# Finishing the last 256 tokens of the last projection as two groups of 128, in another order of products and with stores of 128 KB

## Chip, cores and metric

One core of one Trainium2 chip. The metric is device time in microseconds (us); of several executions the median is given. Each run is compared with the kernel before on its own chip.

## The reference

The computation normalises 2048 tokens of width 1024, runs a dilated local attention (32 heads, window 8) and a SwiGLU block of hidden width 3584 on them, and returns `x + s * g`:

```python
x = A_x
xn = _layernorm(x, axis=-1)
s = _A_ref(xn, A_wqkv, A_wo)          # ... attention, then "@ wo"
g = _silu(_B_ref(xn, B_w1, B_w3, B_w2))
return x + s * g
```

The change touches only the end of this: the projection `@ wo`, the product with the gate `g`, the addition of `x` and the store of the result.

## The kernel before

All large products use seven half-size products in place of eight (Strassen's scheme in Winograd's form): sums of blocks of both operands are made beforehand, seven products run on TensorE into PSUM, and partial results are copied from one PSUM accumulator to another (by ScalarE) or added (by VectorE). Tokens are handled in two batches of 1024 (`b`). Inside `wo`, a batch has two groups of 256 rows in each row half (`gp`), and a group gives four quadrants (`u` for the row half, `dh` for the column half): e11 is (0, 0), e12 is (0, 1), e21 is (1, 0) and e22 is (1, 1). "The last 256 tokens" are the group `b == 1, gp == 1`; strictly it covers 256 rows in each of the two row halves.

For the second batch's last group, VectorE adds `x` and SyncE issues a plain store. The other groups add onto an output that already holds `x`, by an accumulating store from GpSimd.

```python
def wo(b):
    # ... operands; for b == 1 the needed part of x is loaded into xw
        def product(ps, gp, lhs, rhs, first):
            for i in I:
                g = gp * 2 + i
                mm(ps[i], [lhs[:, j, g * P:(g + 1) * P] for j in range(4)], [rhs[:, j, :] for j in range(4)], first)

        both = lambda t: [t[:, i] for i in I]
        for gp in G2:
            run_hooks()
            last = b == 1 and gp == 1
            pa = bank2(f"wa{b}_{gp}")
            product(both(pa), gp, a11, b11, True)
            pe = bank2(f"we{b}_{gp}")
            product(both(pe), gp, s1, t1, True)
            flush()
            pb = [bank2(f"wb{b}_{gp}{i}")[:, i] for i in I] if last else bank2(f"wb{b}_{gp}")
            for i in I:
                if last:
                    act_copy(pb[i], pa[:, i])
            if not last:
                act_copy(pb[:], pa[:])
            pbs = pb if last else both(pb)
            sp5, su2 = k4(f"wsp{b}_{gp}"), k4(f"wsu{b}_{gp}")
            act_copy(sp5[:], pe[:])
            bg((7, 0)[gp] * (1 - b))
            product(pbs, gp, s2, t2, False)
            for i in I:
                if last:
                    act_copy(su2[:, i], pb[i])
            if not last:
                act_copy(su2[:], pb[:])
            product(both(pe), gp, s4, b22, False)
            finished(b, 0, 1, gp, pe, su2[:])
            product(pbs, gp, s3, t3, False)
            finished(b, 1, 1, gp, pb, sp5[:])
            product(both(pa), gp, a12, b21, False)
            finished(b, 0, 0, gp, pa)

            def tail(gp=gp, pb=pb, pbs=pbs):
                product(pbs, gp, a22, t4, False)
                finished(b, 1, 0, gp, pb)

            pend.append(tail)
```

```python
# ... out_rows (the rows of the output that a quadrant's group fills)
    def to_bf16(d, ps, add):
        if add is None:
            nc.scalar.copy(out=d, in_=ps[:])
        elif isinstance(ps, list):
            for i in I:
                nc.vector.tensor_add(d[:, i], ps[i], add[:, i])
        else:
            nc.vector.tensor_add(d, ps[:], add)

    # ...
    def finished(b, u, dh, gp, ps, add=None):
        g = g_tile(b, u, dh, gp)
        n = {(0, 0): 0, (1, 1): 2, (0, 1): 4, (1, 0): 0}[u, dh] + gp
        d = h_sb[:, 16 + 2 * n:18 + 2 * n, CH:]
        rows_ = out_rows(out_flat, b, u, dh, gp)
        with hp():
            if b == 0 or gp == 0:
                to_bf16(d, ps, add)
                anchor["v"] = nc.vector.tensor_mul(g, d, g)
                nc.gpsimd.dma_start(out=rows_, in_=g, accum_op=ALU.add)
            elif (u, dh) != (1, 0):
                to_bf16(d, ps, add)
                nc.vector.tensor_mul(g, d, g)
                nc.vector.tensor_add(g, g, xw[u, dh])
                nc.sync.dma_start(out=rows_, in_=g)
            else:
                for i in I:
                    if i == 0:
                        nc.scalar.copy(out=d[:, i], in_=ps[i])
                    nc.vector.tensor_mul(g[:, i], ps[i] if i else d[:, i], g[:, i])
                    nc.vector.tensor_add(g[:, i], g[:, i], xw[u, dh][:, i])
                    nc.sync.dma_start(out=rows_[:, i], in_=g[:, i])
```

Of the kernel before, what the change touches and what calls it, by code (L numbers as in the profile page):

```python
# [17 lines left out]
def kernel(  # L18
# [11 lines left out]
    nc = tc.nc  # L30
    P = 128
# [4 lines left out]
    CH = 512  # L36
# [9 lines left out]
    I = range(2)  # L46
# [4 lines left out]
    out_flat = out.rearrange("b s d -> (b s) d")  # L51
# [31 lines left out]
        out=ident[:], in_=ident[:], compare_op=ALU.not_equal, fill=1.0,  # L83
# [5 lines left out]
        out=ones4[:], in_=ones4[:], compare_op=ALU.is_ge, fill=0.0,  # L89
# [3 lines left out]
        out=ones4[:], in_=ones4[:], compare_op=ALU.is_ge, fill=0.0,  # L93
# [5 lines left out]
        out=maskb[0:32], in_=maskb[0:32], compare_op=ALU.is_ge, fill=-1.0e9,  # L99
# [7 lines left out]
    h_sb = keep.tile([P, FT, 2 * CH], BF16, name="h_sb")  # L107
# [3 lines left out]
    pb = keep.tile([P, W, P], BF16, name="pb")  # L111
# [20 lines left out]
    def bank2(name):  # L132
        return psum.tile([P, 2, CH], FP32, tag="mm", name=name)

    def k4(name, shape=(2, CH), dt=FP32):
        return kk.tile([P, *shape], dt, tag="k4", name=name)
# [10 lines left out]
    def mm(ps, lhs, rhs, first):  # L147
        n = len(lhs)
        for k in range(n):
            with behind("pe") if "open" in anchor else nullcontext():  # L150
                anchor["pe"] = nc.tensor.matmul(  # L151
                    ps, lhsT=lhs[k], rhs=rhs[k], start=(first and k == 0),
                    stop=(k == n - 1), skip_group_check=not first,
                )
# [4 lines left out]
    def act_copy(out_, in_):  # L159
        with hp():  # L160
            nc.scalar.copy(out=out_, in_=in_)  # L161
# [3 lines left out]
    def flush():  # L165
        while pend:
            pend.pop(0)()
# [51 lines left out]
    anchor = {}  # L219
# [7 lines left out]
    def behind(key):  # L227
        return tc.issue_after(anchor[key].ins) if key in anchor else nullcontext()
# [162 lines left out]
    def att_tile(shape, dt, name):  # L391
        return att.tile([P, *shape], dt, tag="a8", name=name)
# [109 lines left out]
    def run_hooks():  # L502
        while hooks:
            hooks.pop(0)()
# [43 lines left out]
    def bg(us):  # L548
        if us <= 0:
            return  # L550
        state_p[0] = tc.cur_priority
        pace["credit"] += us - pace["owed"]
        pace["owed"] = 0
        with priority(BG), behind("v"):
            while pace["credit"] > 0:
                t = next(att_it)
                if t is STOP:
                    pace["credit"] = min(pace["credit"], 6)
                    break
                else:  # L560
                    pace["credit"] -= t
# [15 lines left out]
    half = [0, 1]  # L577
# [7 lines left out]
    def release(key):  # L585
        free.extend(held.pop(key, []))
# [155 lines left out]
    G2 = range(2)  # L742
    gts = {}

    def g_tile(b, u, dh, gp):
        f0 = {(0, 0): 10, (1, 1): 10, (0, 1): 6, (1, 0): 6}[u, dh] + 2 * gp
        col = {(0, 0): 0, (1, 1): CH, (0, 1): 0, (1, 0): CH}[u, dh]
        return h_sb[:, f0:f0 + 2, col:col + CH]
# [133 lines left out]
    def wo(b):  # L882
        (a11, a12, a21, a22, s1, s2, s3, s4), (b11, b12, b21, b22, t1, t2, t3, t4) = wx[b]
        if b == 1:
            xt4 = att_tile((2, 2, 2, CH), BF16, "xw")
            for u in I:
                for dh in I:
                    xw[u, dh] = xt4[:, u, dh]
                    with behind("dl"):
                        nc.sync.dma_start(out=xw[u, dh], in_=out_rows(x_flat, 1, u, dh, 1))  # L890

        def product(ps, gp, lhs, rhs, first):
            for i in I:
                g = gp * 2 + i
                mm(ps[i], [lhs[:, j, g * P:(g + 1) * P] for j in range(4)], [rhs[:, j, :] for j in range(4)], first)

        both = lambda t: [t[:, i] for i in I]
        for gp in G2:
            run_hooks()
            last = b == 1 and gp == 1  # L900
            pa = bank2(f"wa{b}_{gp}")
            product(both(pa), gp, a11, b11, True)
            pe = bank2(f"we{b}_{gp}")
            product(both(pe), gp, s1, t1, True)
            flush()
            pb = [bank2(f"wb{b}_{gp}{i}")[:, i] for i in I] if last else bank2(f"wb{b}_{gp}")
            for i in I:
                if last:
                    act_copy(pb[i], pa[:, i])
            if not last:  # L910
                act_copy(pb[:], pa[:])
            pbs = pb if last else both(pb)
            sp5, su2 = k4(f"wsp{b}_{gp}"), k4(f"wsu{b}_{gp}")
            act_copy(sp5[:], pe[:])
            bg((7, 0)[gp] * (1 - b))
            product(pbs, gp, s2, t2, False)
            for i in I:
                if last:
                    act_copy(su2[:, i], pb[i])
            if not last:  # L920
                act_copy(su2[:], pb[:])
            product(both(pe), gp, s4, b22, False)
            finished(b, 0, 1, gp, pe, su2[:])
            product(pbs, gp, s3, t3, False)
            finished(b, 1, 1, gp, pb, sp5[:])
            product(both(pa), gp, a12, b21, False)
            finished(b, 0, 0, gp, pa)

            def tail(gp=gp, pb=pb, pbs=pbs):
                product(pbs, gp, a22, t4, False)  # L930
                finished(b, 1, 0, gp, pb)

            pend.append(tail)
        flush()
        release("wo")

    def out_rows(ap, b, u, dh, gp):
        g0 = ((2 * b + u) * NST + gp * 2) * P
        return ap[g0:g0 + 2 * P, dh * CH:(dh + 1) * CH].rearrange("(i p) n -> p i n", p=P)

    def to_bf16(d, ps, add):
        if add is None:
            nc.scalar.copy(out=d, in_=ps[:])
        elif isinstance(ps, list):
            for i in I:
                nc.vector.tensor_add(d[:, i], ps[i], add[:, i])
        else:
            nc.vector.tensor_add(d, ps[:], add)

    xw = {}  # L950

# [5 lines left out]
            with behind("sp"):  # L957
                nc.sync.dma_start(out=out_flat[r0:r0 + n, dh * CH:(dh + 1) * CH], in_=x_flat[r0:r0 + n, dh * CH:(dh + 1) * CH])

    def finished(b, u, dh, gp, ps, add=None):  # L960
        g = g_tile(b, u, dh, gp)
        n = {(0, 0): 0, (1, 1): 2, (0, 1): 4, (1, 0): 0}[u, dh] + gp
        d = h_sb[:, 16 + 2 * n:18 + 2 * n, CH:]
        rows_ = out_rows(out_flat, b, u, dh, gp)
        with hp():
            if b == 0 or gp == 0:
                to_bf16(d, ps, add)
                anchor["v"] = nc.vector.tensor_mul(g, d, g)
                nc.gpsimd.dma_start(out=rows_, in_=g, accum_op=ALU.add)
            elif (u, dh) != (1, 0):  # L970
                to_bf16(d, ps, add)
                nc.vector.tensor_mul(g, d, g)
                nc.vector.tensor_add(g, g, xw[u, dh])
                nc.sync.dma_start(out=rows_, in_=g)
            else:
                for i in I:
                    if i == 0:
                        nc.scalar.copy(out=d[:, i], in_=ps[i])
                    nc.vector.tensor_mul(g[:, i], ps[i] if i else d[:, i], g[:, i])
                    nc.vector.tensor_add(g[:, i], g[:, i], xw[u, dh][:, i])  # L980
                    nc.sync.dma_start(out=rows_[:, i], in_=g[:, i])



# [260 lines left out]
    with behind("dl"):  # L1245
        nc.sync.dma_start(out=xT[:], in_=x_dram[:])
        nc.sync.dma_start(out=xs[:], in_=xs_dram[:])
    wo(0)
    state.add("wo")
    mlp_up(1)  # L1250
    mlp_down(1, lambda: mid(1), (7, 10, 10, 9, 9, 3))
    wo(1)


# [28 lines left out]
```

## Time and profile before

| | kernel before |
|---|---|
| time, median of the first three executions | 723.84 us (723.78 to 724.5) |
| span in the profile | 721.8 us |
| TensorE busy | 710.0 us, 98% |
| first matmul of the last projection | 691.47 us |
| last matmul ends | 715.89 us |
| VectorE's last addition ends | 718.69 us |
| last store: issue begins | 718.85 us |
| end of the span | 721.8 us |

TensorE is busy for 98% of the span and its last matmul ends at 715.89, so what a change at this end can shorten without removing matmuls is the 5.9 us behind it. The prediction below shows the lines of that stretch. What the prediction does not show is how the kernel ends after the last store. The view of the waits on SyncE's queue, behind 717 us (who waited for whom: total in us, times, longest in us), has it:

```profile
SPq L1278 <- DMA out_dram<-h_sb: 1.1, 3, 0.5
SPq L981 <- DVE h_sb L980: 0.3, 1, 0.3
```

The second line is the last store waiting for VectorE's last addition. The first line is the closing of the program on SyncE: it waits until each store has landed, 1.1 us in all, 0.5 the longest. The landing of the last store is therefore part of the time, at full length.

### The profile page before, as it was taken

To read this page: it belongs to the slowest core of one execution; us is meant where nothing else is said; L and a number is where in the kernel's file an instruction comes from. 1 tells how busy PE (TensorE), PEld (TensorE's weight loads), DVE (VectorE), ACT (ScalarE), POOL (GpSimd) and SP (SyncE) were. 2 spreads that over 40 slices of the span, in tenths; PEclk is the share of its full clock that TensorE was granted. 3 is DMA by queue.
4 is the path that set the end of the run, shared out by engine and by line. 5 is a ranking of instruction groups with operands and counts; after the bars stand their busy time and mean duration, and the time that the engine had idled before them with its cause. 6 is when DMAs were issued, how large, how long until landed. Compare 5 with 4: busy or idle time off the path is not lost.

```text
span 721.8 us, 8746 instructions
## 1 busy us (share of the span) xinstructions
PE 710.0 (98%) x3313; PEld 346.2 (48%) x3367; DVE 624.9 (87%) x690; ACT 312.9 (43%) x326; POOL 95.7 (13%) x162
## 2 busy tenths in 40 slices
PE   8999999999999999999999999999999999999996
PEld 6655565654444444444444444444444444444442
DVE  7996879779879878978999999969859989999974
ACT  5745334356545456555555312034364573020233
POOL 0011100012300000233111000000435004000011
PEclk9999999999999999999999999999999999999999
DMA  9946257777754523558756547469799444563615
GB/s 337 275 125 182 82 185 228 258 249 238 246 172 153 191 71 117 173 191 268 246 174 216 190 132 250 144 205 385 168 276 336 139 138 150 168 202 129 199 36 108
DMA packets 119193, 139.51 MB, mean 193 GB/s; under 512 B 17648, under 2 KB 94448, under 8 KB 118512
## 3 DMA queue, kind: packets, MB, share of 16 engines
q1 hardware_dynamic: 104608, 97.01, 42.6%
q0 software_dynamic: 14544, 41.95, 18.0%
q8 instruction: 26, 0.43, 0.2%
q14 instruction: 15, 0.12, 0.1%
HBM read 96.21 MB, written 38.80 MB: 187 GB/s over the span
## 4 chain that ended last, share of the span: by engine, by line
PE 95%; ACT 2%; DVE 2%; issue 1%; DMA 0%; DVEq 0%; ACTq 0%
PE bm L151 20%; PE am L151 13%; PE em L151 13%; PE db L151 10%; PE bq L151 9%; PE de L151 7%; PE da L151 7%; PE eq L151 5%; PE aq L151 3%; PE wb L151 2%; PE af L151 2%; PE we L151 2%; PE wa L151 2%; DVE h_sb L236 1%; PE af L1049 1%
## 5 line engine op out<-in xcount | busy, mean ns | idle before, releaser
L151 PEld LDWEIGHTS <-wring 128*128 128x128 f16 (+1 forms) x1792 | 183.4, 102 | 204.3 <-issue 2.2
L151 PEld LDWEIGHTS <-h_sb 128*128 128x128 f16 (+1 forms) x1056 | 109.5, 104 | 118.4 <-issue 0.6
L151 PE MATMUL bm<-xs,wring 128*128 128x512 f16 x504 | 117.4, 379 | 0.2
L151 PE MATMUL am<-xT,wring 128*128 128x512 bf16 x322 | 79.0, 379 | 0.8
L151 PE MATMUL db<-wring,h_sb 128*128 128x512 f16 x336 | 73.2, 379 | 0.0
L481 DVE TENSOR_TENSOR BC<-Ep,vT 128x2048 bf16<-128x2048 bf16 x56 | 66.6, 1217 | 0.1
L426 DVE TENSOR_TENSOR pt<-qt,kT 128x4096 bf16<-128x4096 bf16 x24 | 54.9, 2290 | 0.6
L664 DVE TENSOR_TENSOR um<-em,um 128x1024 f32<-128x1024 f32 x28 | 34.2, 1222 | 21.0 <-PE em L151 13.3
L666 ACT ACTIVATE g<-um 128x1024 bf16<-128x1024 f32 x28 | 29.6, 1057 | 48.6 <-DVE um L664 48.6
L151 PE MATMUL da<-wring,h_sb 128*128 128x512 bf16 x219 | 48.7, 379 | 0.3
L467 POOL DMA_DIRECT2D Ep<-pb x64 | 38.0, 601 | 53.4 <-DVE pb L463 48.1
L151 PE MATMUL bm<-h_sb,wring 128*128 128x512 f16 x168 | 39.7, 379 | 0.0
L151 PE MATMUL em<-xs,wring 128*128 128x512 f16 x168 | 39.7, 379 | 0.0
L151 PE MATMUL em<-xT,wring 128*128 128x512 bf16 x161 | 39.2, 379 | 0.3
L491 DVE TENSOR_TENSOR oT<-oT,BC 128x2048 bf16<-128x2048 bf16 x32 | 39.0, 1219 | 0.3
L161 ACT COPY bm<-am 128x1024 f32<-128x1024 f32 x28 | 27.9, 998 | 25.9 <-PE am L151 25.9
L161 ACT COPY pm<-em 128x1024 f32<-128x1024 f32 x28 | 28.4, 1013 | 20.1 <-PE em L151 20.1
L161 ACT COPY um<-bm 128x1024 f32<-128x1024 f32 x28 | 28.4, 1014 | 18.9 <-PE bm L151 18.9
L685 ACT CAST g<-bm 128x1024 bf16<-128x1024 f32 x28 | 28.3, 1011 | 17.4 <-PE bm L151 17.4
L679 DVE TENSOR_TENSOR h_sb<-bm,pm 128x1024 bf16<-128x1024 f32 x21 | 25.6, 1218 | 5.1 <-PE bm L151 5.0
L489 DVE TENSOR_TENSOR BC<-BC 128x2048 bf16<-128x2048 bf16 x24 | 29.3, 1221 | 0.4
L428 DVE TENSOR_TENSOR pt<-pt 128x2048 bf16<-128x2048 bf16 x24 | 29.3, 1221 | 0.4
(197 smaller groups left out, 993.5 us busy)
## 6 DMA issues: line engine op xcount, KB each, us to landing
wring<-in_B_w_dram SPq DMA_DIRECT2D x61, 512.0 KB, 4.2
wring<-t_dram SPq DMA_DIRECT2D x16, 512.0 KB, 3.8
t_dram<-wring POOLq DMA_DIRECT2D x14, 512.0 KB, 3.8
wring<-t_dram SPq DMA_DIRECT2D x16, 384.0 KB, 4.9
wring<-in_B_w_dram SPq DMA_DIRECT2D x12, 384.0 KB, 4.5
wring<-in_A_x_dram SPq DMA_DIRECT2D x16, 256.0 KB, 4.2
Ep<-pb POOLq DMA_DIRECT2D x64, 64.0 KB, 4.9
wring<-in_A_wo_dram SPq DMA_DIRECT2D x8, 512.0 KB, 5.6
```

The lines of the kernel that those rows point to most:

```text
L151: anchor["pe"] = nc.tensor.matmul(ps, lhsT=lhs[k], rhs=rhs[k], start=(first and k == 0), stop=(k == n - 1), skip_group_check=not first,)
L161: nc.scalar.copy(out=out_, in_=in_)
L426: nc.vector.tensor_mul(p_t[:], q[:], kT[:, :, o:o + CH])
L428: nc.vector.tensor_add(p_t[:, 0:4, :], p_t[:, 0:4, :], p_t[:, 4:8, :])
L467: nc.gpsimd.dma_start(out=pr[c][r:P:NR, :, sq * P:(sq + 1) * P], in_=pb[sq * 32:(sq + 1) * 32, :, :])
L481: nc.vector.tensor_mul(dst, E[:, w, :].unsqueeze(1).to_broadcast([P, n, CH]), vT[:, js, o:o + CH])
L489: nc.vector.tensor_add(B, B, C)
L491: nc.vector.tensor_add(A, A, B if w0 else C)
L664: v = nc.vector.tensor_add(su2[:], pe[:], su2[:])
L666: nc.scalar.activation(out=hl["g"][:, :, CH:], in_=su2[:], func=ACTF.Silu)
L679: anchor["v"] = nc.vector.tensor_add(h[:, :, CH:], pb[:], sp5[:])
L685: nc.scalar.copy(out=hl["g"][:, :, 0:CH], in_=pb[:])
```

## The change

In the kernel before, the last group of 256 was split only in part: the accumulator `wb` had one PSUM tile for each 128 rows, and the copies around it and the last quadrant were done in halves. The change drops this and runs the last group as two complete groups of 128, so that the quadrants of the first half can be finished while TensorE works on the second. In these two groups e11 comes first, e22 second and e12 third (before: e12, e22, e11). All their stores are plain stores of 128 KB (before: three of 256 KB and two of 128 KB, plain too). The core of the diff (the lines that only pass `ii` on are cut):

```diff
-        def product(ps, gp, lhs, rhs, first):
-            for i in I:
+        def product(ps, gp, ii, lhs, rhs, first):
+            for n, i in enumerate(ii):
...
-        for gp in G2:
+        for gp, ii in ((0, I), (1, I)) if b == 0 else ((0, I), (1, (0,)), (1, (1,))):
...
-            product(both(pe), gp, s4, b22, False)
-            finished(b, 0, 1, gp, pe, su2[:])
-            product(pbs, gp, s3, t3, False)
-            finished(b, 1, 1, gp, pb, sp5[:])
-            product(both(pa), gp, a12, b21, False)
-            finished(b, 0, 0, gp, pa)
+            steps = {
+                "e12": lambda: (product(pe, gp, ii, s4, b22, False), finished(b, 0, 1, gp, ii, pe, su2)),
+                "e22": lambda: (product(pb, gp, ii, s3, t3, False), finished(b, 1, 1, gp, ii, pb, sp5)),
+                "e11": lambda: (product(pa, gp, ii, a12, b21, False), finished(b, 0, 0, gp, ii, pa)),
+            }
+            for k in ("e12", "e22", "e11") if n == 2 else ("e11", "e22", "e12"):
+                steps[k]()
...
+            if add is None:
+                nc.scalar.copy(out=d, in_=ps)
+            else:
+                nc.vector.tensor_add(d, ps, add)
+            anchor["v"] = nc.vector.tensor_mul(g, d, g)
             if b == 0 or gp == 0:
-                to_bf16(d, ps, add)
-                anchor["v"] = nc.vector.tensor_mul(g, d, g)
                 nc.gpsimd.dma_start(out=rows_, in_=g, accum_op=ALU.add)
-            elif (u, dh) != (1, 0):
-                to_bf16(d, ps, add)
-                nc.vector.tensor_mul(g, d, g)
-                nc.vector.tensor_add(g, g, xw[u, dh])
+            else:
+                nc.vector.tensor_add(g, g, xw[u, dh][:, cut])
                 nc.sync.dma_start(out=rows_, in_=g)
-            else:
-                for i in I:
-                    if i == 0:
-                        nc.scalar.copy(out=d[:, i], in_=ps[i])
-                    nc.vector.tensor_mul(g[:, i], ps[i] if i else d[:, i], g[:, i])
-                    nc.vector.tensor_add(g[:, i], g[:, i], xw[u, dh][:, i])
-                    nc.sync.dma_start(out=rows_[:, i], in_=g[:, i])
```

Everything ahead of these groups stands in the same order on every engine in both built programs.

More of the change, by code (lines that the diff above doesn't have):

```diff
@@ L890, in wo @@
                         nc.sync.dma_start(out=xw[u, dh], in_=out_rows(x_flat, 1, u, dh, 1))
-        def product(ps, gp, lhs, rhs, first):
-            for i in I:
+        def product(ps, gp, ii, lhs, rhs, first):
+            for n, i in enumerate(ii):
                 g = gp * 2 + i
-                mm(ps[i], [lhs[:, j, g * P:(g + 1) * P] for j in range(4)], [rhs[:, j, :] for j in range(4)], first)
-        both = lambda t: [t[:, i] for i in I]
-        for gp in G2:
-            run_hooks()
-            last = b == 1 and gp == 1
-            pa = bank2(f"wa{b}_{gp}")
-            product(both(pa), gp, a11, b11, True)
-            pe = bank2(f"we{b}_{gp}")
-            product(both(pe), gp, s1, t1, True)
-            flush()
-            pb = [bank2(f"wb{b}_{gp}{i}")[:, i] for i in I] if last else bank2(f"wb{b}_{gp}")
-            for i in I:
-                if last:
-                    act_copy(pb[i], pa[:, i])
-            if not last:
-                act_copy(pb[:], pa[:])
-            pbs = pb if last else both(pb)
-            sp5, su2 = k4(f"wsp{b}_{gp}"), k4(f"wsu{b}_{gp}")
-            act_copy(sp5[:], pe[:])
-            bg((7, 0)[gp] * (1 - b))
-            product(pbs, gp, s2, t2, False)
-            for i in I:
-                if last:
-                    act_copy(su2[:, i], pb[i])
-            if not last:
-                act_copy(su2[:], pb[:])
-            product(both(pe), gp, s4, b22, False)
-            finished(b, 0, 1, gp, pe, su2[:])
-            product(pbs, gp, s3, t3, False)
-            finished(b, 1, 1, gp, pb, sp5[:])
-            product(both(pa), gp, a12, b21, False)
-            finished(b, 0, 0, gp, pa)
-            def tail(gp=gp, pb=pb, pbs=pbs):
-                product(pbs, gp, a22, t4, False)
-                finished(b, 1, 0, gp, pb)
@@ new lines, in product, with half, tail @@
+                mm(ps[:, n], [lhs[:, j, g * P:(g + 1) * P] for j in range(4)], [rhs[:, j, :] for j in range(4)], first)
+        for gp, ii in ((0, I), (1, I)) if b == 0 else ((0, I), (1, (0,)), (1, (1,))):
+            n = len(ii)
+            name = f"{b}_{gp}{ii[0]}"
+            def half(t):
+                return t[:, 0:n]
+            run_hooks()
+            pa = half(bank2(f"wa{name}"))
+            product(pa, gp, ii, a11, b11, True)
+            pe = half(bank2(f"we{name}"))
+            product(pe, gp, ii, s1, t1, True)
+            flush()
+            pb = half(bank2(f"wb{name}"))
+            act_copy(pb, pa)
+            sp5, su2 = half(k4(f"wsp{name}")), half(k4(f"wsu{name}"))
+            act_copy(sp5, pe)
+            bg((7, 0)[gp] * (1 - b))
+            product(pb, gp, ii, s2, t2, False)
+            act_copy(su2, pb)
+            steps = {
[5 more added lines that the diff above has]
+                steps[k]()
+            def tail(gp=gp, ii=ii, pb=pb):
+                product(pb, gp, ii, a22, t4, False)
+                finished(b, 1, 0, gp, ii, pb)
@@ L939, in out_rows @@
         return ap[g0:g0 + 2 * P, dh * CH:(dh + 1) * CH].rearrange("(i p) n -> p i n", p=P)
-    def to_bf16(d, ps, add):
-        if add is None:
-            nc.scalar.copy(out=d, in_=ps[:])
-        elif isinstance(ps, list):
-            for i in I:
-                nc.vector.tensor_add(d[:, i], ps[i], add[:, i])
-        else:
-            nc.vector.tensor_add(d, ps[:], add)
     xw = {}
@@ L958, in residual, with finished @@
                 nc.sync.dma_start(out=out_flat[r0:r0 + n, dh * CH:(dh + 1) * CH], in_=x_flat[r0:r0 + n, dh * CH:(dh + 1) * CH])
-    def finished(b, u, dh, gp, ps, add=None):
-        g = g_tile(b, u, dh, gp)
+    def finished(b, u, dh, gp, ii, ps, add=None):
+        cut = slice(ii[0], ii[-1] + 1)
+        g = g_tile(b, u, dh, gp)[:, cut]
         n = {(0, 0): 0, (1, 1): 2, (0, 1): 4, (1, 0): 0}[u, dh] + gp
-        d = h_sb[:, 16 + 2 * n:18 + 2 * n, CH:]
-        rows_ = out_rows(out_flat, b, u, dh, gp)
+        d = h_sb[:, 16 + 2 * n:18 + 2 * n, CH:][:, cut]
+        rows_ = out_rows(out_flat, b, u, dh, gp)[:, cut]
         with hp():
+            if add is None:
[3 more added lines that the diff above has]
+            anchor["v"] = nc.vector.tensor_mul(g, d, g)
             if b == 0 or gp == 0:
-                to_bf16(d, ps, add)
-                anchor["v"] = nc.vector.tensor_mul(g, d, g)
                 nc.gpsimd.dma_start(out=rows_, in_=g, accum_op=ALU.add)
-            elif (u, dh) != (1, 0):
-                to_bf16(d, ps, add)
-                nc.vector.tensor_mul(g, d, g)
-                nc.vector.tensor_add(g, g, xw[u, dh])
+            else:
+                nc.vector.tensor_add(g, g, xw[u, dh][:, cut])
                 nc.sync.dma_start(out=rows_, in_=g)
-            else:
-                for i in I:
-                    if i == 0:
-                        nc.scalar.copy(out=d[:, i], in_=ps[i])
-                    nc.vector.tensor_mul(g[:, i], ps[i] if i else d[:, i], g[:, i])
-                    nc.vector.tensor_add(g[:, i], g[:, i], xw[u, dh][:, i])
-                    nc.sync.dma_start(out=rows_[:, i], in_=g[:, i])
     x_load(0)
```

## The prediction

> **What bounds the kernel now.** I read the whole page first, then the chain that ended last, then the last 25 us in order of time, since the change touches only those. The page says that this is a TensorE kernel:
>
> ```profile
> span 721.8 us, 8746 instructions
> PE 710.0 (98%) x3313; PEld 346.2 (48%) x3367; DVE 624.9 (87%) x690; ACT 312.9 (43%) x326; POOL 95.7 (13%) x162
> ...
> PE 95%; ACT 2%; DVE 2%; issue 1%; DMA 0%; DVEq 0%; ACTq 0%
> ```
>
> TensorE is busy for 98% of the span and carries 95% of the chain, so only two things can shorten the time: fewer or faster matmuls, or a shorter stretch at either end in which TensorE has nothing to do. The change adds and removes no matmul (the built programs hold the same number), so what it can win lies after the last matmul. That stretch, in order of time (start, duration, engine, line, operation, output<-inputs, count):
>
> ```profile
> 710.93 1.23 DVE L948 TENSOR_TENSOR h_sb<-we,wsu 128x1024 bf16<-128x1024 f32 x1 [1.99 <-ACT wsu L161]
> 712.07 0.68 DVE L946 TENSOR_TENSOR h_sb<-wb,wsp 128x512 bf16<-128x512 f32 x1
> ...
> 714.00 1.89 PE L151 MATMUL wb<-wring,oT 128*128 128x512 f16 x8
> 714.20 1.01 ACT L943 CAST h_sb<-wa 128x1024 bf16<-128x1024 f32 x1 [3.30 <-PE wa L151]
> ...
> 715.80 0.68 DVE L972 TENSOR_TENSOR h_sb<-h_sb 128x1024 bf16<-128x1024 bf16 x1
> 716.40 0.68 DVE L979 TENSOR_TENSOR h_sb<-wb,h_sb 128x512 bf16<-128x512 f32 x1
> 716.57 0.59 ACT L978 CAST h_sb<-wb 128x512 bf16<-128x512 f32 x1 [1.36 <-DVE h_sb L972]
> 717.00 0.68 DVE L973 TENSOR_TENSOR h_sb<-h_sb,xw 128x1024 bf16<-128x1024 bf16 x1
> 717.60 0.42 DVE L979 TENSOR_TENSOR h_sb<-h_sb 128x512 bf16<-128x512 bf16 x1
> 717.94 0.75 DVE L980 TENSOR_TENSOR h_sb<-h_sb,xw 128x512 bf16<-128x512 bf16 x2
> 718.42 0.84 SPq L981 DMA_DIRECT2D out_dram<-h_sb  x2
> ```
>
> The last matmul ends at 714.00 + 1.89 = 715.89. From there to the end of the span are 5.9 us. VectorE, idle for 1.99 us until 710.93 because no quadrant of the last 256 tokens was complete, then works without a gap to 717.94 + 0.75 = 718.69, which is 2.8 us after TensorE. The last store has been issued by 718.42 + 0.84 = 719.26. The listing of transfers gives 1.8 us from issue to landing for a 128 KB store (2.2 us for 256 KB), so, with the second issue at about 718.9, it lands near 720.7; the remaining 1.1 us are the end of the program. VectorE's backlog is thus the bound of the tail, and ScalarE is not (it even waits 1.36 us for VectorE's L972). The groups by shape give the durations that I use:
>
> ```profile
> L946 DVE TENSOR_TENSOR h_sb<-wb,wsp 128x512 bf16<-128x512 f32 x2 | 1.4, 684 | 0.0
> L972 DVE TENSOR_TENSOR h_sb<-h_sb 128x1024 bf16<-128x1024 bf16 x3 | 2.1, 684 | 0.0
> L980 DVE TENSOR_TENSOR h_sb<-h_sb,xw 128x512 bf16<-128x512 bf16 x2 | 0.8, 416 | 0.0
> L161 ACT COPY wsu<-wb 128x512 f32<-128x512 f32 x2 | 1.2, 590 | 1.1 <-PE wb L151 1.1
> L978 ACT CAST h_sb<-wb 128x512 bf16<-128x512 f32 x1 | 0.6, 586 | 1.4 <-DVE h_sb L972 1.4
> ```
>
> Queued instructions overlap a little: the starts 712.07, 712.67, 713.27 show 0.60 us for an instruction of 0.68, and 717.60 to 717.94 shows 0.34 for one of 0.42.
>
> **What the Trainium skill says.** "VectorE: DVE Perf Modes", section "The perf-mode tier table": an addition or product of two tensors runs at double rate from bf16 in SBUF and at single rate when an operand is in PSUM. The trace agrees: 128x512 costs 416 ns from bf16 but 684 ns with a PSUM operand, the same as 128x1024 from bf16. "ScalarE: Activation LUTs", section "What ACT_TABLE_LOAD costs": 186 ns + 0.833 ns an element, with about 93 ns of overlap back to back. For 512 elements that is 613 ns; the trace has 586 to 590 and decides. "TensorE: Matmul & The Clock Gate", section "Back-to-back issue gap": N/2.4 + 2.5 ns alone, 216 ns for 512 columns; eight matmuls here take 1.73 us, 216 ns each, though the page's lower figure for streams with weight loads (131 ns) does not show here. "DMA: Bandwidth & Descriptors", section "Anatomy of one DMA — SWDGE (gpsimd) path": about 2 us are fixed, mostly waiting for the write receipt, so a smaller store gains little; the 1.8 against 2.2 us above agree.
>
> **The change, part by part.** Each group of tokens needs seven products, whose sums give four quadrants. A quadrant is finished by a copy (ScalarE) or an addition (VectorE) to bf16, a product with the gate, an addition of x, and a store. Before, the last 256 tokens run as one group (56 matmuls) whose quadrants complete one after the other late. Now there are two groups of 28 matmuls (6.04 us each), and within each the order becomes e11, e22, e12, e21. Everything up to the first product for these tokens is unchanged in order on all engines. Batch 0 keeps its groups of 256.
>
> *TensorE.* I laid the new order over 216 ns a matmul, starting as before at 701.83 (700.10 plus eight matmuls), with 0.41 us from the start of a product's last matmul to its consumer (0.38 of duration and 0.03 of wait, as ScalarE's starts show). Halved products cover only 0.86 us each, while a PSUM copy that the next product waits for costs 0.41 + 0.59 + 0.04, less the 0.22 by which the last matmul's start precedes the end of its issue: 0.82. So these waits just fit, except two. In the first half, the ScalarE copy of wb into wsu queues behind the cast of the preceding group; it ends at 706.98 where TensorE wants it at 707.01, so no more than 0.01 is lost. In the second half, the last product waits for the VectorE addition that reads wb (e22): its operand is ready at 714.13, VectorE takes it at 714.22 behind the e11 multiplication, and is done at 714.90, while TensorE would be free at 714.80. That costs 0.14. The old order lost about 0.1 in its own waits (72 matmuls from 700.10 would end at 715.79, not 715.89). The last matmul then ends at about 715.96, 0.07 later than now.
>
> *VectorE.* Per half: two PSUM additions (0.60 each), four multiplications and four additions of x (0.34 each), 3.9 us; for both 7.8, against 7.76 measured now from 710.93 to 718.69. No work is saved. But the first half's quadrants now come from about 707.8 on, in what was idle time, and are done by about 712.9, the last one held back by its product. At the second half: e22 addition 714.22, x to e11 714.82, e12 addition 715.16, then at 715.76 six bf16 instructions of 128x512 remain: 5 x 0.34 + 0.42 = 2.12, end 717.88. Now, at 715.80, there remain three at 0.60, two at 0.34 and a last of 0.42, 2.89 by 718.69 with rounding. **VectorE ends 0.81 us earlier.**
>
> *ScalarE.* Three more instructions (330 against 327 rows), each smaller. The final cast starts at 716.00 and ends at 716.59, before VectorE wants it at 716.78. It costs nothing.
>
> *Stores.* Five become eight, all of 128 KB. Those of the first half are out long before the end. The last two follow VectorE's last two results: e12 ready at 717.54, issued 717.60; e21 ready at 717.88, but the queue spends 0.49 us a store (718.42 to about 718.91), so it is issued at 718.09 instead of 718.91. That is 0.82 earlier, with the same landing of 1.8 us and the same 1.1 us of program end.
>
> Sum: the span falls from 721.8 to about 721.0, and the time from 723.84 to **723.0 us**, 0.1%.
>
> **The rivals.** *New waits on TensorE.* The margins above are a few hundredths of a microsecond. If each of the six or so copy-to-product waits came 0.1 late, TensorE would end 0.6 later and VectorE with it: 723.6. For it: the cover halves with the product. Against it: the copies halve as well, 0.59 against 1.01, and the new order puts e11, which needs no new copy, between a copy and its reader. *TensorE sets the end.* If VectorE kept up fully, the chain from the last matmul would be cast, product, addition: 715.96 + 0.04 + 0.59 + 0.03 + 0.42 + 0.03 + 0.42 = 717.49, 1.2 us better than now, and the time 722.6. Against it: six instructions stand in VectorE's queue at 715.76. *Stores hide it.* More issues at 0.49 each might make the queue the end, or the fixed receipt might stretch with more stores in flight: 723.4 to 723.8. Against it: the last three stores before were 512 KB in 1.5 us, now 384 KB in about 1.2, and the accumulating stores of the earlier group, issued last at 709.24, now come about 1.7 us earlier.
>
> **Range and chances.** All outcomes lie between 722.4 and about 723.8, and the three runs now spread over 0.7 us by themselves. I take 722.3 to 723.9 for 8 in 10. Two per cent is 14 us, more than twice the whole 5.9 us behind the last matmul, so a faster verdict is all but impossible; a slower one needs a disturbance that nothing here suggests.
>
> **What would show it.** In the new profile: the last matmul ends within 0.3 us of 715.9; VectorE's idle wait before the last quadrants breaks into short ones and the first half's stores leave before 714; VectorE's last addition ends near 717.9 and its last six instructions are 416 ns each; the two last stores are issued near 717.6 and 718.1 and land 1.8 us later. The prediction is wrong if TensorE shows gaps of over 0.3 us between the halves, if VectorE's end does not move, or if the distance from its end to the end of the span grows.

## The result, and the profile after

The changed kernel took 723.85 us (723.61 to 723.99, four executions) against 723.84 (723.78 to 724.5). The ratio is 0.9998, with a 95% interval of 0.998 to 1.0015: the same. So the time lies just inside the predicted range, at its upper end, and the gain of 0.8 us that was predicted is not there.

First the head of the page of the changed kernel:

```profile
span 722.2 us, 8818 instructions
PE 713.3 (99%) x3367; PEld 346.2 (48%) x3367; DVE 625.5 (87%) x697; ACT 313.8 (43%) x329; POOL 95.7 (13%) x162
```

TensorE's 713.3 us against 710.0 are no added work. The trace before holds 3313 matmul records to 3367 weight loads, the trace after 3367 to 3367: some records were missing there. Now the end in order of time (start, duration, engine, line, operation, output<-inputs), to be compared with the stretch that the prediction shows:

```profile
714.31 0.43 DVE L959 TENSOR_TENSOR h_sb<-h_sb 128x512 bf16<-128x512 bf16 x1 [0.79 <-ACT h_sb L956]
714.66 0.68 DVE L958 TENSOR_TENSOR h_sb<-wb,wsp 128x512 bf16<-128x512 f32 x1
...
715.39 1.02 PE L151 MATMUL wb<-wring,oT 128*128 128x512 f16 x4
...
715.59 0.68 DVE L958 TENSOR_TENSOR h_sb<-we,wsu 128x512 bf16<-128x512 f32 x1
716.19 0.75 DVE L959 TENSOR_TENSOR h_sb<-h_sb 128x512 bf16<-128x512 bf16 x2
716.50 0.58 ACT L956 CAST h_sb<-wb 128x512 bf16<-128x512 f32 x1 [2.21 <-PE wb L151]
716.86 0.42 DVE L963 TENSOR_TENSOR h_sb<-h_sb,xw 128x512 bf16<-128x512 bf16 x1
717.19 0.42 DVE L959 TENSOR_TENSOR h_sb<-h_sb 128x512 bf16<-128x512 bf16 x1
717.53 0.76 DVE L963 TENSOR_TENSOR h_sb<-h_sb,xw 128x512 bf16<-128x512 bf16 x2
```

This is what the prediction described: VectorE has pauses now, and six bf16 instructions of 128x512 stand at the end, from 716.19 to 717.53 + 0.76 = 718.29. That is 1.9 us behind the last matmul (715.39 + 1.02 = 716.41), where it was 2.8. Yet the span is longer. The following table cuts it where one stage hands over to the next; starts and ends of issues and packets are from the records of the trace, on the clock of the timeline.

| stage (us) | before | after | difference |
|---|---|---|---|
| start to the first matmul of the last projection | 691.47 | 691.89 | +0.42 |
| from there to the end of the last matmul | 24.42 | 24.53 | +0.11 |
| to the end of VectorE's last addition | 2.80 | 1.87 | -0.93 |
| to the begin of the last store's issue | 0.17 | 0.12 | -0.05 |
| to the end of the last store's last packet | 1.42 | 2.36 | **+0.94** |
| to the end of the span | 1.50 | 1.43 | -0.08 |
| span | 721.78 | 722.19 | +0.41 |

Two rows undo the gain: a last store that takes 0.94 longer, and work that reached the last projection 0.42 later although nothing ahead of it was changed. The waits of SyncE's queue behind 717 us in the changed kernel show the first:

```profile
SPq L1261 <- DMA out_dram<-h_sb: 2.0, 2, 1.5
```

The closing waits for stores to land are 2.0 us, the longest 1.5, where they were 1.1 and 0.5. The times from issue to landing of the stores of one line say the same, first of the kernel before (its two stores of 128 KB), then of the changed kernel (all eight):

```profile
DMA to landing us min/median/max: 1.8/1.8/1.8
...
DMA to landing us min/median/max: 1.7/1.7/2.8
```

And the view of the transfers of the changed kernel in the two windows 719 to 720 and 720 to 721 us (forty slices of 25 ns each: busy share of all 16 DMA engines in tenths) shows what the last store does in that time:

```profile
DMA  9989987741105366996999999859220000000000
...
DMA packets 223, 0.20 MB, mean 204 GB/s; under 512 B 31, under 2 KB 222, under 8 KB 222
...
q14 instruction: 1, 0.01, 2.7%
...
DMA  0000101300000300030000020010100000000000
...
DMA packets 9, 0.01 MB, mean 8 GB/s; under 512 B 1, under 2 KB 9, under 8 KB 9
```

At 719.80 nearly everything has been moved. No packet of the store is recorded for 0.31 us, and then nine follow one by one, until 720.76. They are eight of 1 KB and one of 4 bytes, which is a sixteenth of the store (128 packets of 1 KB and 16 of 4 bytes). The landings agree: fifteen of the store's sixteen signals of completion came by 720.15, the sixteenth at 721.23. In the kernel before all sixteen came by 720.62, the last two 0.01 apart. So one share of sixteen was late, and not the whole store. In the first window there is one transfer that is no data: a fetch of instructions on queue 14. Its record says that it began at 719.69, moved 8192 bytes and took 427 ns, to 720.11; the first of the late packets began at 720.11. In the kernel before, the last fetch on this queue came at 723.5, when the span was over. This is a theory that can be tested: **a fetch of instructions took a DMA engine just when the last store needed it.**

### The profile page after: what moved, and what is told of

Same layout as the page of the kernel before. It is cut to its first block, busy times and chain, and to the rows that moved or that the text cites. A ratio compares the mean times of both kernels' runs of the same rounds, so it can differ in the third digit from the quotient of the medians. Undisturbed runs are those within 1.5% of the kernel's fastest.

```text
span 722.2 us, 8818 instructions
## 1 busy us (share of the span) xinstructions
PE 713.3 (99%) x3367; PEld 346.2 (48%) x3367; DVE 625.5 (87%) x697; ACT 313.8 (43%) x329; POOL 95.7 (13%) x162
## 4 chain that ended last, share of the span: by engine, by line
PE 90%; DVE 5%; DMA 2%; ACT 1%; issue 1%; SPq 0%; DVEq 0%; ACTq 0%
PE bm L151 20%; PE am L151 13%; PE em L151 13%; PE bq L151 9%; PE db L151 8%; PE da L151 7%; PE de L151 6%; PE eq L151 5%; PE aq L151 3%; PE wb L151 2%; DVE h_sb L236 2%; PE wa L151 2%; PE we L151 1%; DMA wring<-in_A_x_dram 1%; DMA wring<-in_A_wo_dram 1%
```

## Experiments

**Theory.** VectorE has a few more instructions now (834 recorded entries against 828, waits included), and one of its fetches of instructions, which before fell behind the end, falls on the last store. If the fetch is moved and the kernel kept, the gain should appear.

**Rival 1.** The start of the last projection 0.42 later belongs to the change. **Rival 2.** Eight small stores in place of five land later by themselves. **Rival 3**, for the gain: it is the order of products, or the two groups, or both.

The tool for moving the fetch is a number of one-column memsets on VectorE at the very start, where it waits for its first load. In the traces the other instructions of every engine stand in the same order with and without them:

```diff
     nc.vector.memset(warm[:], 0.0)
+    idle = const.tile([P, 24], FP32, name="idle")
+    for k in range(24):
+        nc.vector.memset(idle[:, k:k + 1], 0.0)
```

Twelve kernels ran, in three batches with five rounds each, and all results were correct. "Before" in the following table is the kernel before in the same batch, nine executions.

| run | median us | before us | ratio (95% interval) | last fetch on queue 14 | last store: issue to last packet |
|---|---|---|---|---|---|
| e1 changed kernel again | 724.03 | 723.84 | 1.0002 (0.9989 to 1.0014) | 719.69 | 2.45 |
| e2 changed, 24 memsets | 722.78 | 723.84 | 0.9988 (0.9975 to 1.0) | 700.5 | 1.41 |
| e3 before, 4 memsets | 724.17 | 723.84 | 1.0006 (0.9992 to 1.0019) | 722.6 | 1.43 |
| e4 before, 24 memsets | 723.97 | 723.84 | 1.0 (0.9988 to 1.0013) | 713.1 | 1.43 |
| e5 before, 7 memsets | 724.36 | 724.0 | 1.0003 (0.9991 to 1.0016) | 719.0 | 1.54 |
| e6 two groups, old order, 24 memsets | 722.27 | 724.0 | 0.9977 (0.9964 to 0.9989) | 708.5 | 1.35 |
| e7 one group, new order, 24 memsets | 724.94 | 724.0 | 1.0013 (1.0 to 1.0026) | 700.6 | 1.96 |
| e8 changed, 24 memsets again | 722.76 | 724.0 | 0.9984 (0.997 to 0.9998) | 700.0 | 1.42 |
| e9 two groups, old order | 722.68 | 724.36 | 0.9977 (0.9963 to 0.999) | 715.2 | 1.34 |
| e10 changed, 4 memsets | 722.89 | 724.36 | 0.9978 (0.9966 to 0.9991) | 714.4 | 1.42 |
| e11 changed, first half's x on GpSimd | 723.63 | 724.36 | 0.9988 (0.9976 to 1.0001) | 723.3 | 1.39 |
| e12 old order, first half's x on GpSimd | 722.65 | 724.36 | 0.9976 (0.9963 to 0.9988) | 721.4 | 1.33 |

Of the differences in time, those of e6, e8, e9, e10 and e12 are clear of the noise by their intervals. Those of e2 and e7 just reach 1 and that of e11 includes it; for these the traces carry the argument, and each trace is of one execution. Three of the fifteen executions of e2, e8 and e10 took 723.4 to 723.6 us; they were not profiled, so it is not known what made them longer.

### e1: the changed kernel again (no edit)

> The changed kernel once more, unedited, as the reference of this batch. Theory (an instruction fetch of VectorE delays the last store): time within 0.4 us of 723.85; the last store again takes about 2.7 us or more to land instead of 1.8, with one fetch of instructions among the transfers between the last issue and the end. Rival 1 (the 0.4 us by which all work was late in the first profile belongs to the change): the last product of the first 256 tokens starts again 0.4 us later than the 700.10 of the kernel before. Theory: that offset is chance of the first load and takes another value.

Measured: 724.03 us. There was a fetch again at 719.69, this time of 607 ns, to 720.30; the first late packet of the store began at 720.30. The fetch ended 0.19 later than in the first trace, and the late packets began 0.19 later. Again one share of sixteen was late: fifteen landings by 720.20, the last at 721.37. The records do not name the DMA engine, so that the fetch and the late share used the same one is inferred from these times. After the fetch the late packets are slow as well (up to 152 ns, against 46 for the others). Packets as slow come after the fetch in e5 (146 ns) and e10 (152 ns) too; I cannot explain it. The test of rival 1 in this run missed: the last projection began at 691.94, so the offset did not take another value. What settles rival 1 are the later traces (see the part on the prediction).

### e2 and e8: the changed kernel with 24 memsets, twice

> The changed kernel with 24 one-column memsets on VectorE at the start, where it waits 2.3 us for the first load. They move VectorE's last fetch of instructions about 24 instructions earlier, away from the last store. Theory: the last store lands in 1.7 to 1.9 us and the time falls by 0.7 to 1.1 us against the changed kernel, to about 723.0. Rival 2 (eight stores of 128 KB in place of five make the landing longer by themselves): landing stays at 2.7 or more, time stays at 723.8. A cost of the memsets themselves would show as a later start of the first statistics, over 3.6 us.

> e2 once more, as the reference of this batch on its chip: 722.5 to 723.1, last store landing in 1.7 to 1.9 us.

Measured: 722.78 and 722.76 us, 1.06 and 1.24 under the kernel before on the same chip. The fetch went to 700 us. It is one of seven of the sixteen fetches on this queue that the 24 memsets of e2 made 12 to 26 us earlier, while the other nine stayed within 2.3 us; that is why I call these seven VectorE's. The view of the transfers in e2 in the windows 719 to 720 and 720 to 721 us, and its closing wait:

```profile
DMA  9989864331556979799998959342100000000000
...
DMA packets 213, 0.19 MB, mean 185 GB/s; under 512 B 32, under 2 KB 213, under 8 KB 213
...
DMA  0000000000000000000000000000000000000000
...
DMA packets 0, 0.00 MB, mean 0 GB/s; under 512 B 0, under 2 KB 0, under 8 KB 0
```

```profile
SPq L1264 <- DMA out_dram<-h_sb: 0.9, 2, 0.5
```

No instruction fetch, no packet behind 720, and the closing wait is back at 0.9. By stages from the start of the last projection, e2 and e8 have 24.53, 1.87, 0.11, then 1.41 and 1.42 in place of 2.36, then 1.31 and 1.32. So rival 2 falls: the eight stores are all there, and the last lands in the old time.

### e4 and e3: the kernel before with 24 and with 4 memsets

> Control: the kernel before with 24 memsets; the fetch moves to before the last stores. Theory and rivals: the time of the kernel before, 723.8, within 0.3; only if the memsets themselves cost something is it longer.

> The kernel before with 4 such memsets. In its trace the last fetch of VectorE's instructions falls 1.8 us behind the end of the span; four instructions more should trigger it near 718.1, so that it moves its 8 KB near 719.8, while the last store is under way. Theory: landing of the last store from 1.8 to about 2.3 to 2.8 us, and the time 0.4 to 1.0 us longer than before, about 724.5. Rival 2: no change, 723.85.

The control came as expected: 723.97 against 723.84, ratio 1.0. No effect of the memsets themselves on the time can be seen, so the gain of e2 is not theirs. (In this trace VectorE ended 3.03 us behind TensorE and not 2.80, because its first addition of the last group began 0.24 later; this is unexplained, and it is a loss.) e3 missed: four memsets moved the fetch from 723.5 only to 722.6, still behind the end of its span (722.0). Its last store was undisturbed, so it tests nothing; the interval of its 724.17 against 723.84 has 1 in it.

### e5: the kernel before with 7 memsets

> The kernel before with 7 memsets. In three traces the fetch was triggered at about the 830th recorded entry of VectorE, 1.5 to 2 us ahead of its 8 KB; four memsets moved that only onto the wait at the closing barrier (fetch at 722.66). With seven, the 830th entry is one of the last additions, near 718.0, so the fetch should come near 719.8, on top of the last store. Theory: last packet of the store at 720.8 to 721.4 instead of 720.3 to 720.5, landing of the last store over 2.3 us, time 0.4 to 1.0 over the kernel before. Rival (the delay needs the eight small stores): landing 1.8, time unchanged.

The fetch came at 719.0 and was over at 719.4, before the last store's issue (719.43) had brought any packets. That store took 1.54 to its last packet, 0.12 longer than before, and the time, 724.36 against 724.0, has 1 in its interval. One of the sixteen landings came 0.17 behind the other fifteen (0.01 in the kernel before), a small delay of the same shape. As a test it is inconclusive: I have not made the kernel before suffer by as much as the changed one does.

### e10: the changed kernel with 4 memsets

> The changed kernel with 4 memsets instead of 24: the fetch should start four entries of VectorE earlier, near 718.5 instead of 719.74, when the data of the last store have not yet come. Theory: one DMA engine is busy for 0.4 us before the last store needs it, so the delay shrinks: landing of the last store 1.7 to 2.3, time 722.7 to 723.5. If the position of the fetch did not matter, it would be the 724.0 of e1; if four memsets did what 24 did by any other way, exactly the 722.8 of e2.

The fetch went to 714.4, much further than the 718.5 that I had worked out from VectorE's entries, and so fully out of the way. The last store took 1.42, the time was 722.89, 1.47 under the kernel before. With the fetch out of the way, 722.89 is what the theory says, but it is also what I had named for the case that memsets help in another way, so e10 alone does not decide between the two. The control e4, in which memsets gained nothing, and e11, which has none, do. My rule for where the fetch falls is not exact. Over the traces it begins 1.5 us or so behind a point between VectorE's recorded entries 821 and 832.

### e11 and e12: no memsets, fewer instructions on VectorE

```diff
-                nc.vector.tensor_add(g, g, xw[u, dh][:, cut])
+                (nc.gpsimd if ii == (0,) else nc.vector).tensor_add(g, g, xw[u, dh][:, cut])
```

> The changed kernel without memsets, the four additions of x of the first 128 tokens on GpSimd: four instructions fewer on VectorE, where it has idle time anyway. Theory: the fetch moves behind the closing barrier as in the kernel before (later than 721), the last store lands in 1.8, time 722.6 to 723.2, as with 24 memsets, which shows that it is where the fetch falls and not the memsets. Rival (landing is the eight stores): 723.9. Risk: GpSimd is slow and disturbs VectorE; then VectorE ends more than 1.9 us behind TensorE.

The fetch moved behind the end (723.3), the last store took 1.39, and the time was 723.63, 0.73 under the kernel before (with 1 in the interval) but over the range that I had given. So the fetch can be moved without memsets, in the other direction, with the same effect on the store. But GpSimd did disturb VectorE, as the risk had named, though it showed in TensorE's end and not, as I had written, in VectorE's distance from it (1.87). Of the trace of e11 in order of time:

```profile
708.98 1.49 POOL L963 TENSOR_TENSOR h_sb<-h_sb,xw 128x512 bf16<-128x512 bf16 x1
709.47 1.29 DVE L959 TENSOR_TENSOR h_sb<-h_sb 128x512 bf16<-128x512 bf16 x1
...
712.55 1.15 POOL L963 TENSOR_TENSOR h_sb<-h_sb,xw 128x512 bf16<-128x512 bf16 x1 [0.41 <-ACT wsp L161]
713.04 0.94 DVE L959 TENSOR_TENSOR h_sb<-h_sb 128x512 bf16<-128x512 bf16 x1 [0.62 <-ACT h_sb L956]
...
716.15 1.02 PE L151 MATMUL wb<-wring,oT 128*128 128x512 f16 x4 [0.45 <-DVE h_sb L958]
```

VectorE's product of 128x512 takes 1.29 and 0.94 us beside an addition on GpSimd, 0.42 alone. The Trainium skill, page "SBUF — State Buffer", section "SBUF: two separate sides", says that VectorE with two inputs in SBUF and GpSimd share a port that one of them holds for a whole instruction; the products end here at 710.76 and 713.98, shortly behind GpSimd's 710.47 and 713.70, which agrees. VectorE falls behind, TensorE waits for VectorE's additions (0.45 before the last product), and its last matmul ends 25.12 behind the start of the projection, not 24.53. That is where about half of the gain went (0.73 against the 1.47 of e10 in the same batch).

> The old order in two groups, with the additions of x of the first 128 tokens on GpSimd and no memsets: the version I would keep. Theory: as e6, 722.0 to 722.6, fetch behind the end.

With the old order the same edit did no such harm (24.71 to TensorE's end, as in e9): 722.65, just over the range given and no better than e9 without it.

### e6, e9 and e7: which part of the change makes the gain

e6 and e9 have two groups of 128 but the old order, e6 with memsets, e9 without:

```diff
-            for k in ("e12", "e22", "e11") if n == 2 else ("e11", "e22", "e12"):
+            for k in ("e12", "e22", "e11"):
```

> The two groups of 128 with the old order of products (e12, e22, e11, then e21), plain stores and 24 memsets: the changed kernel of e2 less its new order. By the durations of the traces: the e12 addition comes 0.9 us earlier, the e22 addition at about the same time, the last product waits about 0.25 for it, and VectorE's queue behind the last matmul shrinks to the e21 product and addition. If the new order is what makes the gain: VectorE ends 2.3 us or more behind TensorE and the time is 0.4 or more over e2. My working: VectorE ends 1.5 to 1.7 behind TensorE (1.87 in e2), time 0 to 0.3 under e2, so the groups alone make the gain.

> The version of e6 without the memsets. It has as many VectorE instructions as the changed kernel, so theory: the fetch triggers near VectorE's end, moves its 8 KB within 2 us of it, on top of the last store, whose landing grows from 1.7 to over 2.3 us; the time is 0.5 to 1.2 over e6, 722.8 to 723.5, and still 0.3 to 0.6 under the changed kernel. Rival (the memsets quicken something else): the last store lands in 1.7 and the gap is elsewhere.

e7 has the new order in one group of 256, with memsets:

```diff
-        for gp, ii in ((0, I), (1, I)) if b == 0 else ((0, I), (1, (0,)), (1, (1,))):
+        for gp, ii in ((0, I), (1, I)):
...
-            for k in ("e12", "e22", "e11") if n == 2 else ("e11", "e22", "e12"):
+            for k in ("e12", "e22", "e11") if b == 0 or gp == 0 else ("e11", "e22", "e12"):
```

> The last 256 tokens as one group, with the new order (e11, e22, e12, then e21), plain stores of 256 KB and 24 memsets: the new order without the split. Expected: the last cast takes 1.01, product and addition 0.68 each, so VectorE ends about 2.6 behind TensorE, the last store of 256 KB lands in 2.2, and the time is 723.6 to 724.1, no better than the kernel before. If the order made the gain, it would be near the 722.8 of e2.

Measured: e6 took 722.27, 0.49 under e8 of its batch, more than the 0 to 0.3 expected; by the stages of the profiled executions it is 0.31. e7 took 724.94, 0.94 over the kernel before. The stages by the profiles:

| stage (us) | before | e8: two groups, new order | e6: two groups, old order | e7: one group, new order |
|---|---|---|---|---|
| last projection to the end of the last matmul | 24.42 | 24.53 | 24.71 | 24.73 |
| to the end of VectorE's last addition | 2.80 | 1.87 | 1.54 | 3.02 |
| to the begin of the last issue | 0.17 | 0.11 | 0.03 | 0.03 |
| to the last packet | 1.42 | 1.42 | 1.35 | 1.96 |
| to the end of the span | 1.50 | 1.32 | 1.31 | 1.61 |
| sum | 30.31 | 29.25 | 28.94 | 31.36 |

The end of e6 in order of time:

```profile
714.58 0.68 DVE L961 TENSOR_TENSOR h_sb<-wb,wsp 128x512 bf16<-128x512 f32 x1
...
715.32 1.02 PE L154 MATMUL wb<-wring,oT 128*128 128x512 f16 x4 [0.16 <-DVE h_sb L961]
...
716.19 0.75 DVE L966 TENSOR_TENSOR h_sb<-h_sb,xw 128x512 bf16<-128x512 bf16 x2
716.38 0.58 ACT L959 CAST h_sb<-wb 128x512 bf16<-128x512 f32 x1 [0.60 <-PE wb L154]
717.00 0.43 DVE L962 TENSOR_TENSOR h_sb<-h_sb 128x512 bf16<-128x512 bf16 x1
717.46 0.43 DVE L966 TENSOR_TENSOR h_sb<-h_sb,xw 128x512 bf16<-128x512 bf16 x1
```

The last product waits 0.16 for the e22 addition, and the last matmul ends 0.18 later than with the new order. But the e12 addition, which the new order leaves for the end, has been made by then. VectorE is out of work at 716.19 + 0.75 = 716.94, a little before the cast ends at 716.96, and behind it stand the product and the addition of e21 alone. TensorE now sets the end: 1.54 us behind the last matmul. That is the chain of the prediction's second rival, cast, product and addition (0.04 + 0.59 + 0.03 + 0.42 + 0.03 + 0.42 = 1.53). And of e7:

```profile
714.72 1.89 PE L154 MATMUL wb<-wring,oT 128*128 128x512 f16 x8 [0.24 <-DVE h_sb L961]
...
717.04 1.38 DVE L962 TENSOR_TENSOR h_sb<-h_sb 128x1024 bf16<-128x1024 bf16 x2
718.34 1.29 DVE L966 TENSOR_TENSOR h_sb<-h_sb,xw 128x1024 bf16<-128x1024 bf16 x2
```

Four full instructions of 128x1024 are left for the end, and the last store has 256 KB and takes 1.96 instead of 1.42 to its last packet. I had expected 723.6 to 724.1; the direction was right, the size was not: VectorE ends 3.02 behind TensorE and not 2.6, TensorE itself 0.3 later. **So the two groups make the gain, and with them the new order gives back 0.2 to 0.5.** (e10 less e9 is 0.21, with executions that overlap, e8 less e6 is 0.49, both within one batch.) One group in the new order wins nothing. What of e7's loss is due to the order is not shown: e7 also lacks the half-size handling of the last quadrant that the kernel before has, and one group in the old order without it was not run.

e9 missed: without memsets its fetch came at 715.2, not on the last store, and its time was below the range given, although it differs from the changed kernel in nothing but the order. It has two recorded entries more on VectorE (836 and 834, waits), which may be why; that was not tested. With its fetch out of the way it needs no memsets. **e9 is the plain version that beats the kernel before**: 722.68 against 724.36 on its chip, 1.68 better. The changed kernel without an edit was not run in that batch; in its own two comparisons it was level with the kernel before.

## Why the prediction was right or wrong

The time lies in the range. But this is luck: the range was wide enough to reach just past the time of the kernel before, and the sum behind it did not hold: 0.84 less was forecast, nothing was found. One of the prediction's own signs of being wrong came true, "if the distance from its end to the end of the span grows": from the end of VectorE's last addition it grew from 3.09 to 3.91 us. By its own steps:

- **TensorE's new waits, 0.07 in sum: held.** Measured 0.11 (24.53 against 24.42), the same in five traces of the new order in two groups. The wait for the e22 addition is there, at the 0.14 predicted (the last product begins at 715.39, and 714.39 + 4 x 0.216 = 715.25). The prediction took the start of the last projection as fixed, however; it was 0.42 later in the first trace. Over the fourteen traces it lies between 691.47 and 692.05; in the four of the kernel before, three of them with memsets, between 691.47 and 692.04, and in e8 of the changed kernel at 691.53. So it is chance and not the change (rival 1 falls). Part of it is there already at the first statistics, which begin at 3.31 in the first trace before and at 3.58 in that after.
- **VectorE ends 0.81 earlier: held.** It is 1.87 behind TensorE, where 717.88 - 715.96 = 1.92 was worked out and 2.80 was measured before; from the start of the last projection it ends 0.82 earlier. No work was saved; it was moved into idle time, as said.
- **The last issue 0.82 earlier: held.** It follows VectorE by 0.12 and comes 0.87 earlier, counted from the start of the last projection.
- **"With the same landing of 1.8 us and the same 1.1 us of program end": this step failed.** The landing took 2.8 us and not 1.8: from issue to last packet the store took 2.36 us (2.45 in e1) in place of 1.42, because a fetch of instructions of VectorE came in between and held up one share of sixteen. With the fetch anywhere else (e2, e8, e10, e11) it took 1.39 to 1.42, so it is neither the number nor the size of the stores. The rival "stores hide it" had named this outcome, with 723.4 to 723.8, but for other reasons: the queue did not become the end, and the landings did not stretch with eight stores (1.76 us from issue to landing in e2). In e2 the first packet of the last store comes 0.90 us after its issue, and the last landing 0.35 us after its last packet.
- **The sum.** With the fetch out of the way the gain was 1.06, 1.24 and 1.47 (e2, e8, e10), somewhat more than the 0.84 forecast. In the stages of e8 the sum is 1.06, of which 0.18 lie between the last packet and the end of the span: 1.31 to 1.33 in the traces of two groups with an undisturbed store, 1.48 to 1.55 in those of the kernel before. I did not expect this and have no cause for it.
- **The order of products**, which the prediction took as a help, helps TensorE by 0.18 and costs VectorE 0.33 (e8 against e6). The prediction did not work out the old order for the same groups; that was an omission, not a wrong number.

What stays open: which of VectorE's entries exactly starts a fetch (e3, e9 and e10 fell elsewhere than expected), why the packets behind the fetch are slow, and whether the kernel before can be hurt by as much (e5 shows 0.12 in the store and nothing clear in the time).

## What to carry to other kernels

At the end of this program the last store counted at full length. So look there not only at the last compute chain but at whatever else may use a DMA engine between the last issue and the last packet, fetches of instructions included; here four memsets more on one engine moved such a fetch by 0.9 us in the one kernel (e3) and 5.3 us in the other (e10), and so out of that stretch in e10. When a gain that the trace shows in one stage is missing in the time, cut both traces at the hand-overs and subtract stage by stage. And when work is split so that its first half hides, look at the order anew: what the second half leaves for the end decides.

## What the Trainium skill lacked or had wrong

- Page "Runtime: NRT & Kernel Launch", section "Instruction fetch mechanics", calls the cost of crossing into the next block of instructions "mostly hidden". It does not say that such a fetch can delay a transfer of data: here 8 KB in 427 and 607 ns, with eight packets of data behind it, made the last store 0.94 and 1.03 us longer.
- The same section gives blocks of 16 KiB. The traces have fetches of 8192 bytes on queue 14 and of 16384 bytes on queue 8; the one that moved with VectorE's instructions has 8192.
- "DMA: Bandwidth & Descriptors" has the queue rows and their turns, but no page says to look for instruction fetches behind the last store. It happened in two of fourteen traces, both of the changed kernel, and cost the whole gain.
- "TensorE: Matmul & The Clock Gate", section "Back-to-back issue gap", gives 131 ns a matmul of 512 columns in a stream with weight loads. Here it is 216 (eight matmuls in 1.73 us).
- "SBUF — State Buffer" says who waits for the port, but no page gives the time that a product takes beside GpSimd. For 128x512 bf16 e11 has 0.89 to 1.29 us in place of 0.42; the four products end 0.28 to 0.29 us after GpSimd's additions.
